# Token mix in three-pass fp32: the half tile of tokens is multiplied with all 128 rows, with zeros in two copies of its weights

## The chip, the cores and the metric

The kernel runs on one core of a Trainium2 chip (all four batches on that core). The metric is the device time of one launch in microseconds. A run with the profiler on gives the times of single instructions; from it come the span (first to last instruction) and the profiled execution's own time.

## The reference, cut to what matters

Three layers stand behind each other: a windowed attention (4 batches, 8 heads, 576 tokens), a channel mix of 512 channels, and a mixer block. The change is in the first half of the mixer block, the token mix:

```python
# x: (4 batches, 576 tokens, 512 channels)
xt = x.transpose(0, 2, 1)
h = np.maximum(xt @ w_tok1, 0.0) @ w_tok2      # w_tok1: 576 x 256, w_tok2: 256 x 576
u = x + h.transpose(0, 2, 1)
h2 = np.maximum(u @ w_ch1, 0.0) @ w_ch2        # 512 x 1536 and 1536 x 512
return u + h2
```

The first product sums over the 576 tokens of a batch. With tokens on the 128 partitions that is four and a half tiles.

## The kernel before, in words

**Arithmetic.** Every large product is made of three matmuls (`mm3`): each operand is split into a high part, rounded to the matmul's input type, and a low part, the rest (`split`: a copy, which the planner gives to ScalarE or VectorE, and a subtraction on VectorE). High times high, high times low and low times high are added up in one PSUM bank.

**Tokens and tiles.** The result of the channel mix lies in 18 tiles `x2[0..17]` of 128 tokens by 512 channels, the batches behind each other. Two batches are nine tiles: four for the even one, four for the odd one, and the ninth, whose rows 0 to 63 are the even batch's last 64 tokens and whose rows 64 to 127 the odd one's. `tiles_of(b)` lists the five tiles of a batch with the rows that count and the number of the weight block.

**Token mix.** `tokens_in(b)` splits each of the five tiles into a pair from the rings `x2h_r`, `x2l_r` (three pairs of 512 columns in z) and multiplies it with w_tok1: 2 halves of the hidden units by 3 matmuls of 512 columns, so 30 matmuls in two banks. For the fifth tile they have 64 rows of the contraction; there are 24 such over the four batches. The weights of the fifth tile lie in `t1[4]`, the tail of w_tok1 twice, once in rows 0 to 63 and once in rows 64 to 127. Then a ReLU gives `hid`. `turn(t)` transposes a tile into `wv` (TensorE, a bank, copies), and `tokens_out(b)` multiplies `hid` with w_tok2 (`t2`, slot at0): 8 groups of 6 matmuls of 288 columns, by turns in banks 6 and 7, each added into `wv` by VectorE. Behind that come the products with w_ch1 (`c1`) and w_ch2 (`c2`).

**Weights.** The weights come as 64-bit words. `weight` loads a block into a raw slot, makes fp32 of it by one ScalarE and three VectorE operations in a temporary slot, and splits it into its high and low place. For w_tok1, w_tok2 and the first four blocks of w_ch1 the raw slots are xt4 and xt5 by turns (`raw_b`), the temporary ones xt6 and xt7 (`tmp_b`). So there are two chains of blocks, the even one over xt4 and xt6, the odd one over xt5 and xt7. The later blocks of w_ch1 and w_ch2 go over wr0 to wr2 and z5 (`raw_c`, `tmp_c`), and wr3, xt4 to xt7 are taken afterwards by the split of u (`uhl_r`).

**What sets the order.** All operations go to a planner (class `Plan`), which records them (so all of them have one line in the profile, L392) and lists them per engine: each gets a due time, worked back from TensorE's own order with a table of costs, and of those that are ready the one with the earliest due time is taken. Two operations that share cells of a slot keep their order. So a change of places or sizes moves instructions on every engine.

The code that sets the places of the token mix:

```python
t1 = [pair(p, (HID,)) for p in cut("at", (1, 2), 512) + [("at", 0, 4 * S), ("at", 0, 4 * S + 512)]]
raw_b, tmp_b = ring(cut("xt", (4, 5), 512)), ring(cut("xt", (6, 7), 512))
x2h_r, x2l_r = ring(z512[9::2]), ring(z512[10::2])
```

Here z512 is z0 to z4 cut into 15 places of 512 columns; z512[8] is the last third of z2, and before the change the token mix doesn't use it.

Of the kernel before, what the change touches and what calls it, by code (L numbers as in the profile page):

```python
# [10 lines left out]
F32R = mybir.dt.float32r  # L11
# [7 lines left out]
B, H, S, D = 4, 8, 576, 64  # L19
C = H * D  # L20
NT = B * S
FF, HID, FF2 = 1024, 256, 1536
# [383 lines left out]
def tile_model(nc, banks, units, cst, mu, w_k, w_v, w_r, w_t1, w_t2, w_c1, w_c2, outT):  # L406
    memory = {k: [Slot(f"{k}{i}", n) for i, n in enumerate(v)] for k, v in SLOTS.items()}

    def f(view):
        return view.bitcast(F32)  # L410

    def at(place, shape, dtype=F32):
        name, number, offset = place
        return memory[name][number].view(offset, shape, dtype)
# [6 lines left out]
    def cut(name, numbers, size, count=None):  # L421

        out = []
        for n in numbers:
            out += [(name, n, size * i) for i in range(SLOTS[name][n] // size)]
        return out[:count]

    def ring(*places):
        return Ring(at, sum((p if isinstance(p, list) else [p] for p in places), []))

    def psum(*numbers):
        return Ring(bank, numbers)

    def mm3(out, lh, ll, rh, rl, first, last):

        nc.tensor.matmul(out=out, lhsT=lh, rhs=rh, start=first, stop=False)
        nc.tensor.matmul(out=out, lhsT=lh, rhs=rl, start=False, stop=False)
        nc.tensor.matmul(out=out, lhsT=ll, rhs=rh, start=False, stop=last)

    def copy(out, in_):  # L440
        nc.either(
            ("scalar", "activation", dict(out=out, in_=in_, func=AF.Copy)),
            ("vector", "tensor_copy", dict(out=out, in_=in_)),
        )

    def combine(out, in0, in1, op):
        nc.vector.tensor_tensor(out=out, in0=in0, in1=in1, op=op)

    def split(raw, hi, lo):
        copy(hi, raw)  # L450
        combine(lo, raw, f(hi), ALU.subtract)

    def rows(n):
        return slice(128 * n, 128 * n + 128)
# [6 lines left out]
    def pair(place, shape):  # L461

        name, number, offset = place
        n = int(np.prod(shape))
        return at(place, shape, F32R), at((name, number, offset + n), shape, F32R)
# [3 lines left out]
    wr = [pair(("wr", k, 0), (C,)) for k in range(4)]  # L469
# [3 lines left out]
    def words(w):  # L473
        return w.bitcast(U32)
# [2 lines left out]

        return words(w).rearrange("(k p) c -> p k c", p=128)[:, :, 2 * n * m:2 * n * m + 2 * n]

    def weight(srcs, hi, lo, raw_ring, tmp_ring):  # L480

        shape = tuple(hi.shape[1:])
        n = int(np.prod(shape))  # L490
        flat = raw_ring.tile(2 * n, dtype=U32)
        for part, src in srcs:
            dst = flat[part]
            if len(src.shape) == 3:
                dst = dst.split(src.shape[1], src.shape[2])
            nc.sync.dma_start(out=dst, in_=src)
            if raw_ring is raw_a:
                nc.early[len(nc.ops) - 1] = 6
        raw = flat.split(n, 2)
        low, h = raw[:, :, 0], raw[:, :, 1]  # L500
        t = tmp_ring.tile(n)
        b, half = t.bitcast(U32), t.bitcast(U16)
        v = nc.vector
        nc.scalar.activation(out=t, in_=f(h), func=AF.Copy, scale=2.0 ** -112)
        v.tensor_scalar(out=h, in0=b, scalar1=3, scalar2=None, op0=ALU.logical_shift_left)
        v.scalar_tensor_tensor(
            out=b, in0=b, scalar=0x80000000, in1=h, op0=ALU.bitwise_and, op1=ALU.bitwise_or
        )
        v.scalar_tensor_tensor(
            out=half, in0=low, scalar=2.0 ** -29, in1=half, op0=ALU.mult, op1=ALU.add  # L510
        )
        if len(shape) == 2:
            t = t.split(*shape)
        split(t, hi, lo)
# [4 lines left out]
    def weight_k(m):  # L519

        weight([(everything, col_block(w_k, m, 256))], *wk2[m], raw_a, tmp_a)

    def weight_r(kt):
        weight([(everything, words(w_r)[rows(kt), :])], *wr[kt], raw_a, tmp_a)

    def weight_v(m):

        two = words(w_v)[256 * m:256 * m + 256, :].rearrange("(k p) c -> p k c", p=128)
        weight([(everything, two)], *wv2[m], raw_a, tmp_a)
# [88 lines left out]
    z512 = cut("z", range(5), 512)  # L618
# [4 lines left out]
    x2 = [at(place, (C,)) for place in x2_at]  # L623
# [63 lines left out]
    def mix(c, m, j):  # L687
# [16 lines left out]
        out=om_sb, in0=mu_sb, scalar1=-1.0, scalar2=1.0, op0=ALU.mult, op1=ALU.add  # L704
    )
    diag = []
    for which in range(2):
        diag.append([])
        for kt in range(4):
            diag[which].append([])  # L710
            for k, factor in enumerate((om_sb, mu_sb)):
# [3 lines left out]
                        out=d, in0=ident, scalar1=factor[:, col], scalar2=None, op0=ALU.mult)),  # L715
# [19 lines left out]
    for g in range(8 * nchunk + 2):  # L735
        c, m = divmod(g, 8)
# [29 lines left out]
            attend(h, s_ring, t_ring, x_ring)  # L766


    t1 = [pair(p, (HID,)) for p in cut("at", (1, 2), 512) + [("at", 0, 4 * S), ("at", 0, 4 * S + 512)]]
    t2 = [pair(p, (S,)) for p in cut("at", (0,), 2 * S, 2)]  # L770
    raw_b, tmp_b = ring(cut("xt", (4, 5), 512)), ring(cut("xt", (6, 7), 512))
    for k in range(4):
        weight([(everything, words(w_t1)[rows(k), :])], *t1[k], raw_b, tmp_b)
    tail = words(w_t1)[512:576, :]
    weight([(slice(0, 64), tail), (slice(64, 128), tail)], *t1[4], raw_b, tmp_b)
    for k in range(2):
        for n in range(3):
            cs = slice(192 * n, 192 * n + 192)
# [12 lines left out]
    x2h_r, x2l_r = ring(z512[9::2]), ring(z512[10::2])  # L791
# [4 lines left out]
    def weight_1(m):  # L796
        if m < 4:
            for n in range(2):
                q = slice(2 * n, 2 * n + 2)
                weight([(everything, col_block(w_c1, m)[:, q, :])], c1[m][0][:, q, :], c1[m][1][:, q, :], raw_b, tmp_b)  # L800
        else:
            weight([(everything, col_block(w_c1, m))], *c1[m], raw_c, tmp_c)
# [3 lines left out]

    def tiles_of(b):
        base, odd = 9 * (b // 2), b % 2
        out = [(base + 4 * odd + i, slice(0, 128), i) for i in range(4)]
        return out + [(base + 8, slice(64 * odd, 64 * odd + 64), 4)]  # L810

    for m in range(4):
        weight_1(m)
    hid = {}
    hp_r, x2p_r, up_r = psum(0, 1, 2, 3), psum(4, 5), psum(6, 7)

    def tokens_in(b):
        hp = [hp_r.tile(C) for _ in range(2)]
        for n, (t, r, kt) in enumerate(tiles_of(b)):
            h, l = x2h_r.tile(C, dtype=F32R), x2l_r.tile(C, dtype=F32R)  # L820
            split(x2[t][r], h[r], l[r])
            for m in range(2):
                mm3(hp[m], t1[kt][0][r, rows(m)], t1[kt][1][r, rows(m)], h[r], l[r], n == 0, n == 4)
        hid[b] = []
        for m in range(2):
            h, l = (hid_r.tile(C, dtype=F32R) for _ in range(2))
            nc.scalar.activation(out=h, in_=hp[m], func=AF.Relu)
            nc.vector.scalar_tensor_tensor(
                out=l, in0=hp[m], scalar=0.0, in1=f(h), op0=ALU.max, op1=ALU.subtract
            )  # L830
            hid[b].append((h, l))
# [25 lines left out]
    for t in range(4):  # L857
        turn(t)
    tokens_in(0)
    turn(8)  # L860
    for t in range(4, 8):
        turn(t)
    tokens_in(1)
    tokens_out(0)
    for t in range(9, 13):
        turn(t)
    tokens_in(2)
    turn(17)
    tokens_out(1)
# [59 lines left out]
    for g in range(12 * nchunk + 2):  # L929
        c, m = divmod(g, 12)  # L930
# [90 lines left out]
```

## Time and profile before

| | us |
|---|---|
| median of 3 runs | 734.55 |
| lowest, highest | 733.45, 735.19 |
| profiled execution, its own time | 732.79 |
| span of the profiled execution | 731.0 |
| TensorE busy in the span | 715.6 (98%) |
| VectorE busy | 404.7 (55%) |
| ScalarE busy | 287.1 (39%) |

The granted clock of TensorE, as a mean over the span, is 0.989 of full. The token mix lies between 362 and 430 us of the span. In TensorE's timeline a row gives its start and length; rows of like neighbours are joined. The length of a row runs past the start of the next one, since matmuls overlap, so an instruction's price is read from start to start.

### The profile page before, as it was taken

The numbers are of one execution on the slowest core, as the hardware profiler recorded it, in microseconds if no ns is written. First come the engines' busy times: TensorE is split into PE (matmuls) and PEld (weight loads), VectorE is DVE, ScalarE is ACT, GpSimd is POOL, SyncE is SP. The second block draws the span as 40 slices with busy tenths as digits, with TensorE's granted clock in tenths as the row PEclk, the third lists the DMA queues.
The fourth block names the chain that finished last, engine by engine and source line by source line (L and its number), as shares of the span: only waits on it lengthen the run. The fifth ranks groups of instructions, "written<-read, shape, count | busy, mean of one in ns | idle before, by whom it ended". The sixth has DMA issues, their size and how long they took to land.

```text
span 731.0 us, 10615 instructions
## 1 busy us (share of the span) xinstructions
PE 715.6 (98%) x4124; PEld 604.6 (83%) x4124; DVE 404.7 (55%) x917; ACT 287.1 (39%) x803; POOL 1.2 (0%) x20
## 2 busy tenths in 40 slices
PE   7699999999999999999999999999999999999998
PEld 6578888888888888988878888888888888888897
DVE  6898898387477388786788898132114112211121
ACT  5776775356244354464466543120112011011110
POOL 0000000000000000000000000000000000000000
PEclk9799999999999999999999999999999999999999
DMA  8946632214122100203321342001000000100010
GB/s 293 323 156 225 196 132 81 67 52 144 47 68 70 46 16 22 73 30 105 98 81 54 96 127 76 1 0 58 1 0 23 35 1 1 57 1 0 1 59 30
DMA packets 26082, 53.84 MB, mean 74 GB/s; under 512 B 2480, under 2 KB 10032, under 8 KB 26032
## 3 DMA queue, kind: packets, MB, share of 16 engines
q1 hardware_dynamic: 26032, 53.17, 22.9%
q8 instruction: 32, 0.52, 0.3%
q14 instruction: 18, 0.15, 0.1%
HBM read 48.44 MB, written 4.72 MB: 73 GB/s over the span
## 4 chain that ended last, share of the span: by engine, by line
PE 95%; DMA 4%; SPq 0%; issue 0%; DVE 0%
PE bank L392 95%; DMA at<-units 2%; DMA wr<-units 1%; DMA wv<-units 1%; SPq L392 0%; DVE z L392 0%
## 5 line engine op out<-in xcount | busy, mean ns | idle before, releaser
L392 PE MATMUL bank<-z,wk 128*128 128x384 f32 (+2 forms) x816 | 196.4, 358 | 0.0
L392 DVE SCALAR_TENSOR_TENSOR z<-bank,z 128x512 fp32r<-128x512 f32 (+2 forms) x116 | 70.4, 607 | 222.3 <-ACT z L392 221.5
L392 ACT ACTIVATE z<-bank 128x512 fp32r<-128x512 f32 (+3 forms) x123 | 65.0, 529 | 285.3 <-PE bank L392 284.3
L392 PEld LDWEIGHTS bank<-z,wk 128*128 128x128 f32 x816 | 146.9, 188 | 15.1 <-ACT x L392 0.3
L392 PE MATMUL bank<-wv,z 128*128 128x512 f32 x432 | 128.9, 405 | 0.0
L392 PE MATMUL bank<-z,x 128*128 128x512 f32 (+1 forms) x540 | 120.2, 371 | 0.0
L392 PEld LDWEIGHTS bank<-z,x 128*128 128x128 f32 x540 | 94.9, 188 | 18.7
L392 PEld LDWEIGHTS bank<-wv,z 128*128 128x128 f32 x432 | 78.3, 189 | 13.8
L392 PE MATMUL bank<-z,at 128*128 128x512 f32 (+2 forms) x300 | 76.9, 388 | 0.0
L392 PE MATMUL bank<-wr,z 128*128 128x512 f32 x216 | 62.8, 406 | 0.0
L392 PEld LDWEIGHTS bank<-z,at 128*128 128x128 f32 (+1 forms) x300 | 52.6, 188 | 11.3 <-issue 1.3
L392 PE MATMUL bank<-at 128*128 128x96 f32 (+1 forms) x252 | 46.3, 284 | 11.0 <-DMA at<-cst 4.9
L392 ACT ACTIVATE at<-bank,at 128x96 f32<-128x96 f32 x128 | 42.4, 340 | 23.7 <-PE bank L392 11.6
L392 DVE TENSOR_TENSOR z<-z,z 128x384 fp32r<-128x384 f32 x88 | 48.1, 554 | 5.8 <-ACT z L392 2.6
L392 PE MATMUL bank<-xt,wk 128*128 128x512 f32 (+2 forms) x176 | 45.2, 387 | 0.0
L392 PEld LDWEIGHTS bank<-wr,z 128*128 128x128 f32 x216 | 39.2, 189 | 6.6
L392 PEld LDWEIGHTS bank<-at 128*128 128x128 f32 x216 | 35.3, 195 | 8.0 <-DMA at<-units 4.1
L392 PE MATMUL bank<-at,z 128*128 128x288 f32 x192 | 35.9, 306 | 0.0
L392 PEld LDWEIGHTS bank<-xt,wk 128*128 128x128 f32 x176 | 30.5, 192 | 6.1
L392 ACT ACTIVATE z<-z 128x384 fp32r<-128x384 f32 x57 | 29.5, 522 | 14.3 <-DVE z L392 8.3
L392 ACT ACTIVATE x<-bank 96x512 f32<-96x512 f32 (+1 forms) x41 | 24.2, 594 | 27.1 <-PE bank L392 26.9
L392 PEld LDWEIGHTS bank<-at,z 128*128 128x128 f32 x192 | 29.7, 188 | 4.0 <-issue 1.8
(106 smaller groups left out, 787.2 us busy)
## 6 DMA issues: line engine op xcount, KB each, us to landing
at<-units SPq DMA_DIRECT2D x27, 416.0 KB, 3.7
wr<-w_c SPq DMA_DIRECT2D x20, 512.0 KB, 3.6
at<-units SPq DMA_DIRECT2D x27, 192.0 KB, 2.6
x<-w_k SPq DMA_DIRECT2D x4, 1024.0 KB, 6.9
x<-w_v SPq DMA_DIRECT2D x4, 1024.0 KB, 7.0
wv<-units SPq DMA_DIRECT2D x8, 416.0 KB, 6.6
outT<-z SPq DMA_DIRECT2D x9, 256.0 KB, 2.0
x<-w_r SPq DMA_DIRECT2D x4, 512.0 KB, 3.6
```

The lines of the kernel that those rows point to most:

```text
L392: call(kw["out"], kw["constant"]) if method == "memset" else call(**kw)
```

## The change

`weight` gets a parameter `zero`: the rows it names are set to zero in the raw slot, by a memset on GpSimd. The tail of w_tok1 becomes two blocks in place of one: `t1[4]` with the tail in rows 0 to 63 and zeros below, `t1[5]` with zeros in rows 0 to 63 and the tail below. The sixth pair lies in z512[8]. The fifth tile of a batch is multiplied with all 128 rows, by `t1[4]` for an even batch and `t1[5]` for an odd one. Its split is made for all 128 rows, once for two batches, at a place in wr3 (`ends`), no longer in the rings.

```diff
+        if zero is not None:
+            nc.gpsimd.memset(out=f(flat[zero]), constant=0.0)
...
-    t1 = [pair(p, (HID,)) for p in cut("at", (1, 2), 512) + [("at", 0, 4 * S), ("at", 0, 4 * S + 512)]]
+    t1 = [pair(p, (HID,)) for p in cut("at", (1, 2), 512) + [("at", 0, 4 * S), ("at", 0, 4 * S + 512), z512[8]]]
...
-    weight([(slice(0, 64), tail), (slice(64, 128), tail)], *t1[4], raw_b, tmp_b)
+    halves = [slice(0, 64), slice(64, 128)]
+    for odd in range(2):
+        weight([(halves[odd], tail)], *t1[4 + odd], raw_b, tmp_b, zero=halves[1 - odd])
...
-        out = [(base + 4 * odd + i, slice(0, 128), i) for i in range(4)]
-        return out + [(base + 8, slice(64 * odd, 64 * odd + 64), 4)]
+        return [(base + 4 * odd + i, i) for i in range(4)] + [(base + 8, 4 + odd)]
...
-        for n, (t, r, kt) in enumerate(tiles_of(b)):
-            h, l = x2h_r.tile(C, dtype=F32R), x2l_r.tile(C, dtype=F32R)
-            split(x2[t][r], h[r], l[r])
+        for n, (t, kt) in enumerate(tiles_of(b)):
+            if n < 4:
+                h, l = x2h_r.tile(C, dtype=F32R), x2l_r.tile(C, dtype=F32R)
+            elif b % 2 == 0:
+                h, l = ends[b // 2] = at(("wr", 3, 0), (C,), F32R), at(("wr", 3, 512), (C,), F32R)
+            else:
+                h, l = ends[b // 2]
+            if n < 4 or b % 2 == 0:
+                split(x2[t], h, l)
             for m in range(2):
-                mm3(hp[m], t1[kt][0][r, rows(m)], t1[kt][1][r, rows(m)], h[r], l[r], n == 0, n == 4)
+                mm3(hp[m], t1[kt][0][:, rows(m)], t1[kt][1][:, rows(m)], h, l, n == 0, n == 4)
```

The order of the instructions moves with it. TensorE, half tile of batch 3 (z3, z4, wr3: halves of the tile, the moving operand; at0, z2: weights of the tail; the rows on bank6 and bank7 are tokens_out of batch 2), before:

```order
L392 MATMUL bank7_68<-at0_1_2633,z0_0_526 128x288 x2
L392 MATMUL bank2_63<-z3_0_474,at0_1_2633 128x512
L392 MATMUL bank7_68<-at0_1_2633,z0_0_526 128x288
L392 MATMUL bank2_63<-z4_1_532,at0_1_2633 128x512
L392 MATMUL bank7_68<-at0_1_2633,z0_0_526 128x288 x2
L392 MATMUL bank2_63<-z3_0_474,at0_1_2633 128x512
L392 MATMUL bank7_68<-at0_1_2633,z1_0_580 128x288
L392 MATMUL bank3_64<-z3_0_474,at0_1_2633 128x512
L392 MATMUL bank3_64<-z4_1_532,at0_1_2633 128x512
L392 MATMUL bank3_64<-z3_0_474,at0_1_2633 128x512
L392 MATMUL bank6_67<-at0_1_2633,z0_0_526 128x288 x5
```

The same place after:

```order
L392 MATMUL bank7_68<-at0_1_2628,z0_0_526 128x288 x2
L392 MATMUL bank2_63<-wr3_1_585,z2_0_434 128x512
L392 MATMUL bank7_68<-at0_1_2628,z0_0_526 128x288
L392 MATMUL bank2_63<-wr3_1_585,z2_0_434 128x512
L392 MATMUL bank7_68<-at0_1_2628,z0_0_526 128x288 x2
L392 MATMUL bank2_63<-wr3_1_585,z2_0_434 128x512
L392 MATMUL bank7_68<-at0_1_2628,z1_0_580 128x288
L392 MATMUL bank3_64<-wr3_1_585,z2_0_434 128x512 x3
L392 MATMUL bank6_67<-at0_1_2628,z0_0_526 128x288 x5
```

The sequence is the same, matmul for matmul; the half tile's operands come from wr3 and z2, with all rows.

SyncE's queue, loads of the token mix's weights (xt4, xt5: raw slots; w_t1, w_t2, w_c1, w_c2: w_tok1, w_tok2, w_ch1, w_ch2), before:

```order
L392 DMA xt4_0_83<-w_t1 64x512 x2
L392 DMA xt5_0_85<-w_t2 128x384
L392 DMA xt4_0_83<-w_t2 128x384
L392 DMA xt5_0_85<-w_t2 128x384
L392 DMA xt4_0_83<-w_t2 128x384
L392 DMA xt5_0_85<-w_t2 128x384
L392 DMA xt4_0_83<-w_t2 128x384
L392 DMA xt5_0_85<-w_c1 128x2x256
L392 DMA xt4_0_83<-w_c1 128x2x256
L392 DMA xt5_0_85<-w_c1 128x2x256
```

The same place after:

```order
L392 DMA xt4_0_83<-w_t1 64x512
L392 DMA xt5_0_85<-w_t1 64x512
L392 DMA xt4_0_83<-w_t2 128x384
L392 DMA xt5_0_85<-w_t2 128x384
L392 DMA xt4_0_83<-w_t2 128x384 x2
L392 DMA xt4_0_83<-w_c1 128x2x256 x4
L392 DMA wr2_2_3096<-w_c1 128x4x256
L392 DMA wr0_2_3112<-w_c2 128x1024
L392 DMA wr1_2_3128<-w_c2 128x1024
L392 DMA xt5_0_85<-w_t2 128x384 x2
L392 DMA wr0_2_3112<-w_c2 128x1024
L392 DMA xt5_0_85<-w_c1 128x2x256
```

The loads of xt5 move behind those of xt4 and behind three of wr.

ScalarE, at the last chunk of the channel mix (x24, x25: tiles of its result; z5 to z4: the mix of the last chunk; xt6, xt7: temporary slots of the two chains), before:

```order
L392 ACTIVATE x24_0_188<-bank0_61 128x512
L392 ACTIVATE xt6_0_79<-xt4_0_83 128x256
L392 ACTIVATE z5_0_513<-bank1_62 128x384
L392 ACTIVATE xt7_0_81<-xt5_0_85 128x256
L392 ACTIVATE xt2_1_3122<-xt6_0_79 128x256
L392 ACTIVATE z4_1_532<-z5_0_513 128x384
L392 ACTIVATE z3_0_474<-x25_0_685 128x512 x2
L392 ACTIVATE x24_0_188<-bank2_63 128x512
```

The same place after:

```order
L392 ACTIVATE x24_0_188<-bank0_61 128x512
L392 ACTIVATE xt6_0_79<-xt4_0_83 128x256
L392 ACTIVATE z5_0_513<-bank1_62 128x384
L392 ACTIVATE z2_0_434<-xt7_0_81 128x256
L392 ACTIVATE z4_1_532<-z5_0_513 128x384
L392 ACTIVATE z3_0_474<-x25_0_685 128x512
L392 ACTIVATE xt7_0_81<-xt5_0_85 128x192
L392 ACTIVATE z3_0_474<-x25_0_685 128x512
L392 ACTIVATE x24_0_188<-bank2_63 128x512
```

The odd chain is at its second tail block (the write into z2) and its first piece of w_tok2 where it was at the last pieces of w_ch1.

## Rows read from the trace of the kernel before

**Rows 1.** The page: busy time of each engine, chain that ended last.

```profile
PE 715.6 (98%) x4124; PEld 604.6 (83%) x4124; DVE 404.7 (55%) x917; ACT 287.1 (39%) x803; POOL 1.2 (0%) x20
PE 95%; DMA 4%; SPq 0%; issue 0%; DVE 0%
```

**Rows 2.** TensorE's timeline, half tile of batch 3 (start us, us, engine, operands).

```profile
415.27 0.42 PE L392 MATMUL bank<-at,z 128*128 128x288 f32 x2
415.62 0.50 PE L392 MATMUL bank<-z,at 64*128 64x512 f32 x1
...
416.38 0.49 PE L392 MATMUL bank<-z,at 64*128 64x512 f32 x1
...
418.01 0.97 PE L392 MATMUL bank<-z,at 64*128 64x512 f32 x3
418.91 1.86 PE L392 MATMUL bank<-at,z 128*128 128x288 f32 x12
420.61 0.86 PE L392 MATMUL bank<-xt,xt 128*128 128x512 f32 x3
```

**Rows 3.** TensorE's timeline, two stretches of like matmuls.

```profile
426.44 1.75 PE L392 MATMUL bank<-at,z 128*128 128x288 f32 x12
428.04 0.39 PE L392 MATMUL bank<-wr,xt 128*128 128x512 f32 x1
...
485.31 2.92 PE L392 MATMUL bank<-z,at 128*128 128x512 f32 x12
488.07 2.94 PE L392 MATMUL bank<-z,xt 128*128 128x512 f32 x12
```

**Rows 4.** Its ends of the stretches of batches 0, 1, 2; the form's group.

```profile
369.11 1.59 PE L392 MATMUL bank<-z,at 128*128 128x512 f32 x5
...
372.12 0.76 PE L392 MATMUL bank<-cst,x 128*128 128x128 f32 x5
372.64 1.18 PE L392 MATMUL bank<-z,at 128*128 128x512 f32 x4
...
379.85 1.76 PE L392 MATMUL bank<-z,at 128*128 128x512 f32 x6
...
384.49 0.38 PE L392 MATMUL bank<-cst,x 128*128 128x128 f32 x2
...
396.34 1.75 PE L392 MATMUL bank<-z,at 128*128 128x512 f32 x6
...
399.28 0.27 PE L392 MATMUL bank<-cst,x 128*128 128x128 f32 x1
...
L392 PE MATMUL bank<-z,at 64*128 64x512 f32 x24 | 8.8, 444 | 0.0
```

**Rows 5.** Windows: us, busy PE, PEld, DVE, ACT, POOL, PEclk, DMA share, GB/s.

```profile
343.00:362.00 19.00, 19.00 (x97) 16.64 (x96) 13.07 (x28) 7.72 (x16) 0.00 (x0) 1.00 0.35 112
362.00:430.00 68.00, 68.00 (x392) 57.00 (x391) 58.82 (x111) 42.13 (x95) 0.00 (x0) 1.00 0.28 86
430.00:470.00 40.00, 40.00 (x174) 32.50 (x173) 25.74 (x48) 12.90 (x22) 0.00 (x0) 1.00 0.23 67
```

**Rows 6.** TensorE's timeline: last receptance matmul; first tokens_out matmuls.

```profile
344.71 0.40 PE L392 MATMUL bank<-wr,z 128*128 128x512 f32 x1
...
376.88 0.42 PE L392 MATMUL bank<-at,z 128*128 128x288 f32 x2
```

**Rows 7.** Groups by form, whole span (busy, mean ns; idle before, releaser).

```profile
L392 DVE TENSOR_TENSOR z<-x,z 64x512 fp32r<-64x512 f32 x4 | 2.7, 685 | 0.4 <-ACT z L392 0.4
L392 DVE SCALAR_TENSOR_TENSOR xt<-xt,xt 128x256 uint16<-128x256 uint32 x13 | 5.6, 450 | 0.2
L392 POOL MEMSET xt<- 128x1 f32 x16 | 1.1, 111 | 57.1 <-PE bank L392 56.8 <-POOLq L1005 0.3
```

**Rows 8.** The page: DMA issues (count, KB each, median us to landing).

```profile
wr<-w_c SPq DMA_DIRECT2D x20, 512.0 KB, 3.6
xt<-w_t SPq DMA_DIRECT2D x6, 192.0 KB, 2.4
```

More of the change, by code (lines that the diff above doesn't have):

```diff
@@ L478, in col_block, with weight @@
         return words(w).rearrange("(k p) c -> p k c", p=128)[:, :, 2 * n * m:2 * n * m + 2 * n]
-    def weight(srcs, hi, lo, raw_ring, tmp_ring):
+    def weight(srcs, hi, lo, raw_ring, tmp_ring, zero=None):
         shape = tuple(hi.shape[1:])
@@ L808, in tiles_of @@
         base, odd = 9 * (b // 2), b % 2
-        out = [(base + 4 * odd + i, slice(0, 128), i) for i in range(4)]
-        return out + [(base + 8, slice(64 * odd, 64 * odd + 64), 4)]
+        return [(base + 4 * odd + i, i) for i in range(4)] + [(base + 8, 4 + odd)]
     for m in range(4):
         weight_1(m)
-    hid = {}
+    hid, ends = {}, {}
     hp_r, x2p_r, up_r = psum(0, 1, 2, 3), psum(4, 5), psum(6, 7)
```

## The prediction

> **What bounds the kernel now.** I read the page first, for the engine that sets the end. TensorE is busy for 98% of the span and the chain that ended last is 95% TensorE [rows 1]. Then I read the windows over the stretch that the change touches, 343 to 430 us: TensorE is busy 19.00 of 19 us and 68.00 of 68, at a granted clock of 1.00 [rows 5]. It never waits there, so only what makes its own instructions take less time, or what makes it wait for the first time, can move the end. Busy time alone does not say what an instruction costs, since the records of neighbours overlap. So I read TensorE's timeline from start to start.
>
> In a stretch of like instructions the price is steady. Twelve 512-column matmuls take 485.31 to 488.07, which is 0.230 us each; twelve of 288 columns take 426.44 to 428.04, 0.133 each [rows 3]. Now the half tile of batch 3 [rows 2]. A 64-row matmul starts at 415.62, and after one 288-column matmul of 128 rows the next 64-row one starts at 416.38. That pair takes 0.76 us where 0.230 + 0.133 = 0.363 would do: 0.40 us too much. The extra time is not in the 64-row matmul as such: three of them in a row take 418.01 to 418.91, 0.90 us for 0.69, so 0.21 too much on three; the rest of the 0.4 falls on the neighbours of 128 rows. It hangs on the passage from 128 rows to 64 and back. The reader is to see a fixed price for each run of 64-row matmuls, however long the run.
>
> **The change, part by part.**
>
> *The half tiles get all 128 rows.* The 24 matmuls stay 24, of 512 columns each [rows 4]; there is none less. But no run of 64 rows is left, so all passages go. The sum, stretch by stretch, is start to start less what the same instructions cost in the uniform stretches. (A row of the timeline joins neighbours and carries the form of the first; the order of the program gives the counts within.)
> - Batch 3, 415.27 to 420.61: 5.34 us. In it 18 matmuls of 288 columns and 6 of 512: 18 × 0.133 + 6 × 0.230 = 3.77. Excess 1.57, in 4 runs [rows 2].
> - Batch 1, 379.85 to 384.49: 4.64 us, with 8 of 512 and 12 of 288, 3.44. Excess 1.20, in 3 runs [rows 4].
> - Batch 2, 396.34 to 399.28: 2.94 us, with 7 of 512 and 4 of 288, 2.14. Excess 0.80, in 2 runs [rows 4].
> - Batch 0, 369.11 to 372.64: 3.53 us, with 7 of 512 (1.61) and 8 transposes. Five transposes at the end take 372.12 to 372.64, 0.104 each, so 0.83. Excess 1.09, in 3 runs [rows 4].
>
> Together 4.66 us for 12 runs, 0.39 a run; I take 4.65. It lies wholly on the path, since TensorE does nothing else in that time. What could make it smaller is that 128 rows cost more than 64 in themselves. Within the run of three the price is that of a full matmul plus one passage, so I take none. The bounds are all of the excess, and half of it, if only one side of each passage vanished.
>
> The Trainium skill, "TensorEngine Tiling (Array Packing)", section "Theoretical Speedup", says that a contraction of 64 rows or fewer can run up to twice as fast when the array is split into tiles. By that rule a 64-row matmul would be worth 0.115 us less than a full one, and the 24 would lose 2.8 us of the gain by being widened. The row of three at 418.01 shows no such halving [rows 2]. So the sum goes by the row; the rule stands among the rivals.
>
> *One split per pair of batches.* Four half-tile splits become two. Each removed one saves 0.685 us of VectorE [rows 7] and a copy on ScalarE or VectorE. TensorE waits for none of them, so it is worth nothing by itself; it is relief for VectorE of 1.37 us.
>
> *A second copy of the tail weights.* The tail is loaded as two single pieces in place of two parts of one slot, so no byte is added; there is one more conversion (one ScalarE operation, three on VectorE, a copy and a subtraction). Each is at most 0.45 us by the dearest of its kind [rows 7], except that the subtraction of 256 columns lies below the 0.685 of 512. It comes on ScalarE and VectorE while TensorE is busy throughout [rows 5]. Cost 0 with that cover; without it, some 2.25 us once.
>
> *Two memsets of 64x512 on GpSimd.* No such memset is in the trace. From below: 0.11 us for 128x1 [rows 7]; from above: 0.685 us, what VectorE takes for a subtraction of 64x512 [rows 7], doubled for a slower engine, 1.4. I take 1.0, near the upper end, since the form is that of the upper row. GpSimd has nothing else here, and the load of the other half of the same slot, of 128 KB, lasts some 2.4 us by the row of 192 KB [rows 8], so the cost is 0 at either end.
>
> *A wait that is new.* The second copy lies in a part of z2 that holds an operand of the last receptance. Its last matmul starts at 344.71 and takes 0.40 [rows 6], so the copy can be written from about 345.1. Behind it hangs one of the two chains of raw and temporary buffers: three of the six pieces of w_tok2, then four halves of the first w_ch1 blocks. On ScalarE the conversion of the mix and two tile copies for batch 0 stand behind the waiting copy; in SyncE's queue two of the three pieces now stand behind three 512 KB loads of wr.
> When are they ready? The copy and subtraction end by 346.4 (2 × 0.685 at most). Three wr loads add 3.6 us [rows 8]. A step of the chain is a load of 2.4 [rows 8] and five operations of at most 0.45 [rows 7], 2.25: some 4.7 us. So 346.4 + 3.6 + 3 × 4.7 = 364.1. The first tokens_out matmul, which reads w_tok2, starts at 376.88 [rows 6], and at 375.8 when batch 0 has lost its 1.09. There are 11.7 us to spare; cost 0, and if the cover were gone, whatever the steps exceed.
>
> *VectorE in 362 to 430.* It is busy 58.82 of 68.00 us [rows 5]. The four halves of w_ch1 that come later bring at most 4 × 4 × 0.45 = 7.2 us, the removed splits take away 1.37: 64.65. The stretch shrinks to 68.00 − 4.65 = 63.35. So it would be 1.3 us over full. Much of that work, though, converts blocks of w_ch1 and w_ch2 that are used later, and in 430 to 470 VectorE is busy only 25.74 of 40 [rows 5]. I take it to slip there, cost 0. This is the weakest step: an addition of tokens_out that stands behind two conversions in the queue would hold a PSUM bank, and TensorE with it.
>
> **The sum.** The profiled execution took 732.79 us (span 731.0) and lies 1.76 below the median of 734.55. Less 4.65 it would be 728.1 (span 726.35). The median becomes 734.55 − 4.65 = 729.9; from the lowest and highest run, 728.8 and 730.5.
>
> **The rivals.**
> 1. VectorE gives part of it back. For it: 64.65 us of work in 63.35. Against it: less than that is urgent. It gives back 1.3 us at least; if the queue also stands still for a twentieth of a stretch of some 35 us around tokens_out, 3. Time 731.2 to 732.9.
> 2. Only one side of each passage vanishes, or the wider matmul costs something. For it: no row shows a 128-row half tile. Against it: the uniform rows. Half of 4.65 stays: 732.2.
> 3. A 64-row matmul is in truth cheaper, by half, and its price is hidden behind the passages. The change then gains 4.65 − 24 × 0.115 = 1.9: 732.7. Against it: the row of three. This is what the rule of the Trainium skill above would do.
> 4. Slower. The second copy's wait starves tokens_out. The chain must be later than 375.8: from 346.4 + 3.6 that is a step of over 8.6 us; the whole gain is lost over 10.2. At 11 us a step TensorE waits 383 − 375.8 = 7.2, and the time is 734.55 + 2.55 = 737.1. For it: three more transfers ahead in the queue, and VectorE nearly full. Against it: a step by rows is 4.7.
> 5. More gain than summed: the first matmuls of other stretches also change neighbours, or the relief of ScalarE counts. 728.5.
> That the change does nothing on TensorE is excluded by the order: none of its rows there is a 64-row one.
>
> **How the numbers follow.** Chances: forecast 0.69, rival 1 0.19, rival 2 0.04, rival 3 0.02, rival 4 0.04, rival 5 0.02. The forecast with the spread of the runs covers 728.8 to 730.5; I let the range begin at 728.6 and reach to 732.5, which takes in most of rivals 1 and 2 and leaves about 0.15 outside. Within 0.2% (1.5 us) is about what a measurement of this kernel can tell from no change; 733.1 is that bound. Faster is nearly all of the forecast and of rivals 1, 2, 3 and 5: 0.90. Same is a rival 1 that gives back over 3 us, or rival 4 near its turning point: 0.06. Slower 0.04.
>
> **What would show it.** In the changed profile TensorE's timeline should show 0.230 and 0.133 us start to start through tokens_in of all four batches, and no row with 64 rows. The four stretches should take 3.77, 3.44, 2.14 and 2.44 us. TensorE should be busy throughout 343 to 425. Wrong would be: idle time on TensorE ahead of the first tokens_out matmuls, released by VectorE on at0 (rival 4) or on a bank that a VectorE addition frees (rival 1); or half-tile matmuls more than 0.235 us apart in a stretch of their like (rivals 2, 3).

## The result, and the profile after

The changed kernel took 728.32 us (median of 4 runs, 727.19 to 728.68) against 734.87 for the kernel before in the same comparison: ratio 0.9911, 95% interval 0.9893 to 0.9929. That is 6.5 us less where 4.65 were forecast, and 0.3 us below the range. In two later comparisons with more runs the ratio was 0.9925 (0.990 to 0.995) and 0.9937 (0.9917 to 0.9956); the forecast 4.65 us is 0.9937. How much of the first difference lay in the runs of before is told apart below.

The page of the profile after: span, busy time of each engine, chain that ended last. They answer to [rows 1].

```profile
span 725.4 us, 10621 instructions
PE 709.9 (98%) x4124; PEld 604.4 (83%) x4124; DVE 405.3 (56%) x922; ACT 285.3 (39%) x800; POOL 2.3 (0%) x22
PE 94%; DMA 3%; DVE 1%; ACT 0%; SPq 0%; issue 0%
```

TensorE has the same 4124 matmuls and 5.7 us less busy time. Its timeline through the half tile of batch 3 in the changed kernel (start us, us, operands), which answers to [rows 2]:

```profile
411.25 0.43 PE L392 MATMUL bank<-at,z 128*128 128x288 f32 x2
411.52 0.39 PE L392 MATMUL bank<-wr,z 128*128 128x512 f32 x1
411.75 0.29 PE L392 MATMUL bank<-at,z 128*128 128x288 f32 x1
411.88 0.39 PE L392 MATMUL bank<-wr,z 128*128 128x512 f32 x1
...
412.74 0.86 PE L392 MATMUL bank<-wr,z 128*128 128x512 f32 x3
413.43 1.75 PE L392 MATMUL bank<-at,z 128*128 128x288 f32 x12
415.02 0.63 PE L392 MATMUL bank<-xt,xt 128*128 128x512 f32 x2
```

From 411.52 to 411.88 a 512-column and a 288-column matmul take 0.36 us, where the pair with 64 rows took 0.76. The whole stretch, 411.25 to 415.02, takes 3.77 us, to the hundredth what the sum had for it; before it took 5.34.

Windows of the changed kernel (us, busy PE, PEld, DVE, ACT, POOL, granted clock, DMA share, GB/s), which answer to [rows 5]:

```profile
343.00:362.00 19.00, 19.00 (x99) 16.66 (x98) 14.79 (x35) 9.02 (x22) 0.00 (x0) 1.00 0.47 145
362.00:425.40 63.40, 63.40 (x389) 57.11 (x388) 58.14 (x118) 41.57 (x96) 0.00 (x0) 1.00 0.29 88
```

TensorE still does not wait. VectorE is busy for 58.14 of 63.40 us: fuller than before (58.82 of 68.00), but not full.

To tell the token mix from everything else I take two fixed points of TensorE's timeline: the last matmul of the receptance, ahead of the token mix, and a run of twelve matmuls (the first on at0 as a weight of w_ch2) behind it. In the profile before they stand at 344.71 [rows 6] and 485.31 [rows 3], 140.60 us apart. After:

```profile
343.73 0.40 PE L392 MATMUL bank<-wr,z 128*128 128x512 f32 x1
...
479.70 2.92 PE L392 MATMUL bank<-z,at 128*128 128x512 f32 x12
```

They are 135.97 us apart, 4.63 less. The remaining 0.98 of the 5.6 us between the two profiles lies ahead of the first point. Matched instruction by instruction, the two timelines part by it within the first 100 us, where both programs have the same instructions in the same order on every engine, and by no more from there to the first point.

| stretch of the half tile | before, us | summed for after | measured after |
|---|---|---|---|
| batch 0 | 3.53 | 2.44 | 2.50 (368.15 to 370.65) |
| batch 1 | 4.64 | 3.44 | 3.47 (377.83 to 381.30) |
| batch 2 | 2.94 | 2.14 | 2.13 (393.15 to 395.28) |
| batch 3 | 5.34 | 3.77 | 3.77 (411.25 to 415.02) |

### The profile page after: what moved, and what is told of

It is laid out like the page before. It is cut to its first block, busy times and chain, and to the rows that moved or that the text cites. A ratio compares the mean times of both kernels' runs of the same rounds, so it can differ in the third digit from the quotient of the medians.

```text
span 725.4 us, 10621 instructions
## 1 busy us (share of the span) xinstructions
PE 709.9 (98%) x4124; PEld 604.4 (83%) x4124; DVE 405.3 (56%) x922; ACT 285.3 (39%) x800; POOL 2.3 (0%) x22
## 4 chain that ended last, share of the span: by engine, by line
PE 94%; DMA 3%; DVE 1%; ACT 0%; SPq 0%; issue 0%
PE bank L392 94%; DMA x<-w_v 1%; DMA wr<-units 1%; DMA wv<-units 1%; DVE x L392 1%; SPq L392 0%; DVE at L392 0%; ACT x L392 0%; ACT wk L392 0%; DVE z L392 0%; ACT at L392 0%
## 5 line engine op out<-in xcount | busy, mean ns | idle before, releaser
L392 PE MATMUL bank<-z,at 128*128 128x512 f32 (+1 forms) x276 | 68.9, 383 | 0.0
L392 PE MATMUL bank<-wr,z 128*128 128x512 f32 x228 | 66.6, 406 | 0.0
L392 PEld LDWEIGHTS bank<-z,at 128*128 128x128 f32 x276 | 48.4, 188 | 8.6
L392 PEld LDWEIGHTS bank<-wr,z 128*128 128x128 f32 x228 | 41.4, 189 | 7.0
```

Source lines behind the costliest of these rows:

```text
L392: call(kw["out"], kw["constant"]) if method == "memset" else call(**kw)
```

## The experiments

Theory A: a passage between matmuls of 64 and of 128 rows has a fixed price, some 0.39 us for a run of 64-row matmuls, and that is the whole gain. Rivals: the single split or the moved chains bring a part; the 64-row matmul itself is dear; or the change also shortens the start.

The distance between the two fixed points, from one profile of each kernel, carries most of the verdicts:

| kernel | first point | second | distance | against before |
|---|---|---|---|---|
| before, first profile | 344.71 | 485.31 | 140.60 | |
| before, second profile | 346.81 | 488.95 | 142.14 | +1.54 |
| before, third profile | 344.87 | 485.44 | 140.57 | -0.03 |
| changed, first profile | 343.73 | 479.70 | 135.97 | -4.63 |
| changed, second profile | 343.68 | 479.89 | 136.21 | -4.39 |
| changed, third profile | 343.34 | 479.30 | 135.96 | -4.64 |
| changed, 64 rows again | 346.68 | 487.23 | 140.55 | -0.05 |
| before, full rows alone | 346.18 | 482.17 | 135.99 | -4.61 |
| before, runs of six | 347.06 | 484.54 | 137.48 | -3.12 |
| before, all tiles 64 rows | 344.98 | 513.55 | 168.57 | +27.97 |
| the same in 8 runs | 345.12 | 483.87 | 138.75 | -1.85 |
| paired halves | 347.17 | 482.24 | 135.07 | -5.53 |
| paired halves, early | 344.33 | 478.38 | 134.05 | -6.55 |

### 1. Both kernels once more

No edit.

> The kernel before once more, unchanged, for the spread of the first 100 us, where both kernels run the same instructions and the profile after is nevertheless 0.97 us ahead. Theory A, chance of the start: this profile too is shifted against the first one of before by some tenths of a us up to 1 us within the first 100 us and by nothing after that; ratio 1.000. Theory B, the start belongs to the program: the shift in the first 100 us is under 0.1 us and the ratio is 1.000.

> The changed kernel once more, unchanged. Theory A, only the passages count and the rest of the measured 6.5 us was the start: in more rounds the ratio comes down towards 0.9937 (4.65 us less), and this profile is 4.64 us shorter than before between 362 and 435 us, with another shift in the first 100 us. Theory B, the change also makes the start shorter: the ratio stays at 0.991 (6.5 us less) and the first 100 us are again about 1 us shorter.

Measured: the kernel before 733.25 us (12 runs) against 733.98 (29 runs) for itself, ratio 0.9995 (0.9974 to 1.0016); the changed one 728.49 (6 runs), ratio 0.9925 (0.990 to 0.995). The first point, ahead of the token mix, stood at 344.71 in the first profile of before and at 346.81 in the second: the same program starts 2.1 us later or earlier. That is theory A of the start, though beyond the 1 us it allowed. The ratio of the changed kernel lies between its two theories, and its start was again 1 us ahead, as theory B wanted; number 7 comes back to it.

The second profile of before had something else, which neither theory foresaw. Two fixed points are 142.14 us apart, 1.54 too many. Windows behind the half tile of batch 3 in it:

```profile
400.00:420.00 20.00, 20.00 (x121) 17.21 (x120) 16.67 (x33) 12.61 (x30) 0.00 (x0) 1.00 0.32 95
420.00:422.00 2.00, 2.00 (x8) 1.47 (x8) 1.65 (x3) 1.61 (x4) 0.00 (x0) 0.75 0.34 114
422.00:424.00 2.00, 2.00 (x10) 2.00 (x9) 1.05 (x2) 0.10 (x1) 0.00 (x0) 0.50 0.00 0
```

and the timeline rows in it, TensorE, with the last 64-row run and what follows:

```profile
420.11 0.97 PE L392 MATMUL bank<-z,at 64*128 64x512 f32 x3
421.02 3.25 PE L392 MATMUL bank<-at,z 128*128 128x288 f32 x12
424.06 1.04 PE L392 MATMUL bank<-xt,xt 128*128 128x512 f32 x3
```

The twelve 288-column matmuls take 3.04 us from start to start where they took 1.70 in the first profile [rows 2]. The granted clock stood at 0.50, the lower of its two levels (1.2 GHz in place of 2.4). It came down after four runs of 64-row matmuls in 5 us, and TensorE never waited.

### 2. The changed kernel with 64 rows again

```diff
-                mm3(hp[m], t1[kt][0][:, rows(m)], t1[kt][1][:, rows(m)], h, l, n == 0, n == 4)
+                r = slice(0, 128) if n < 4 else halves[b % 2]
+                mm3(hp[m], t1[kt][0][r, rows(m)], t1[kt][1][r, rows(m)], h[r], l[r], n == 0, n == 4)
```

> The changed kernel with its two copies, its single split and its order of loads, but the half tile multiplied with 64 rows again. Theory A, the passages between 64 and 128 rows are the gain: 12 runs of 64-row matmuls are back, so 4.65 us come back, 362 to 435 us as long as before, ratio about 1.000. Rival, the single split and the moved chains bring a part of the gain: ratio 0.994 to 0.997, and the stretch stays 2 to 4 us shorter than before.

Measured: 733.76 us (12 runs), ratio 1.000 (0.9979 to 1.0021); the distance is 140.55, as before. The single split, the second copy and the moved chains are all in this kernel, and none of the gain is. TensorE at batch 3 of it:

```profile
417.58 0.50 PE L392 MATMUL bank<-wr,z 64*128 64x512 f32 x1
418.01 0.40 PE L392 MATMUL bank<-at,z 128*128 128x288 f32 x1
418.34 0.49 PE L392 MATMUL bank<-wr,z 64*128 64x512 f32 x1
```

The pair takes 0.76 us again, now with the operands in wr3 and z2: the price belongs to the rows, not to the place.

### 3. The kernel before with full rows alone

```diff
-        return out + [(base + 8, slice(64 * odd, 64 * odd + 64), 4)]
+        return out + [(base + 8, slice(0, 128), 4)]
```

> The kernel before with its order and its one copy of the tail weights, but each half tile split and multiplied with all 128 rows, so that both batches' last tokens go into the sum of either: the separation of the two batches is left out. Theory A, the passages alone: 4.65 us less between 362 and 435 us as in the changed kernel, ratio 0.9937. Rival, the second copy and the moved chains bring part of it: less than 4 us.

Measured: 729.40 us (4 runs), ratio 0.9937 (0.9918 to 0.9956), distance 135.99. With 2 it closes the question from both sides: rows alone give 4.61 us, and all the rest of the change moves the distance by no more than 0.05 us.

### 4. Runs of six

```diff
+            start = len(nc.ops)
             for m in range(2):
                 mm3(hp[m], t1[kt][0][r, rows(m)], t1[kt][1][r, rows(m)], h[r], l[r], n == 0, n == 4)
+            if n == 4:
+                nc.burst(start)
```

> The kernel before with the six 64-row matmuls of a batch kept together, so 4 runs of six in place of 12 runs; nothing else is changed. Theory A, a fixed price of 0.39 us a run: 8 x 0.39 = 3.1 us less, ratio 0.9957. Rival, each 64-row matmul costs 0.19 us more than one of 128 rows: no gain, ratio 1.000.

Measured: 730.41 us (12 runs), ratio 0.9952 (0.9937 to 0.9967), distance 137.48: 3.12 less, against 8 x 0.39 = 3.1 expected. TensorE at the half tile of batch 0 in it:

```profile
371.32 0.49 PE L392 MATMUL bank<-cst,x 128*128 128x128 f32 x3
371.74 1.66 PE L392 MATMUL bank<-z,at 64*128 64x512 f32 x6
373.33 0.77 PE L392 MATMUL bank<-cst,x 128*128 128x128 f32 x5
```

Six 64-row matmuls from 371.74 to 373.33 take 1.59 us for 6 x 0.230 = 1.38: 0.21 too much for six, as for three and for one. The price hangs on the run, not on the matmul; the rival of a dear 64-row matmul falls.

### 5. All tiles by 64 rows: does the clock come down?

```diff
-        out = [(base + 4 * odd + i, slice(0, 128), i) for i in range(4)]
+        out = [(base + 4 * odd + i, slice(64 * odd, 64 * odd + 64), i) for i in range(4)]
```

> The kernel before with all five tiles of each batch multiplied by 64 rows only (rows 0 to 63 for an even batch, 64 to 127 for an odd one), so half of the tokens are left out of the first product; the number and order of the matmuls stay. Theory A, 0.39 us a run: 47 runs in place of 12, 35 x 0.39 = 13.7 us more, ratio 1.019, with the granted clock at 1.00 from 362 to 430. Theory C, 64-row matmuls also bring the granted clock down, as it stood at 0.50 behind batch 3 in the second profile of before: the clock lies at 0.50 in one or more stretches between 362 and 430 us, and the kernel is slower by 16 us or more, ratio 1.022 or above.

Measured: 765.46 us (4 runs, 761.01 to 775.00, with mean granted clocks from 0.969 down to 0.951), ratio 1.0436 (1.0391 to 1.048). The profiled run is the shortest, with 28 us more between the fixed points where 35 runs more would cost 13.7. Windows of it:

```profile
362.00:380.00 18.00, 18.00 (x78) 11.48 (x78) 13.37 (x24) 12.34 (x30) 0.00 (x0) 1.00 0.19 59
380.00:400.00 20.00, 20.00 (x78) 14.14 (x77) 11.09 (x22) 8.91 (x18) 0.00 (x0) 0.74 0.08 26
400.00:420.00 20.00, 20.00 (x71) 14.08 (x71) 10.49 (x20) 8.05 (x17) 0.00 (x0) 0.74 0.26 79
420.00:450.00 30.00, 30.00 (x116) 20.53 (x115) 17.20 (x32) 11.00 (x24) 0.00 (x0) 0.77 0.23 71
450.00:480.00 30.00, 30.00 (x150) 25.41 (x149) 27.61 (x55) 13.30 (x23) 0.00 (x0) 1.00 0.35 106
```

The clock lay at its full level up to 380, had a mean of 0.74 to 0.77 for 70 us, and was full again behind the token mix. In these 70 us (380 to 450) the lost clock alone is 20 x 0.26 + 20 x 0.26 + 30 x 0.23 = 17.3 us, where 28.0 - 13.7 = 14.3 are to be explained. The sum does not close to better than 3 us, but by either count the clock accounts for half of the 28 us or more.

### 6. The same matmuls in 8 runs: rows or passages?

```diff
+        for part in (range(3), range(3, 5)):
...
+            start = len(nc.ops)
+            for n, (r, kt, h, l) in pairs.items():
+                for m in range(2):
+                    mm3(hp[m], t1[kt][0][r, rows(m)], t1[kt][1][r, rows(m)], h[r], l[r], n == 0, n == 4)
+            nc.burst(start)
```

> The kernel with all five tiles on 64 rows (half the tokens left out, as there), but the 30 matmuls of a batch kept in one run of 18 and one of 12, so 8 runs in place of 47. If the granted clock falls because of the 64 rows, it lies at 0.50 in some stretch between 362 and 430 us here too, and the kernel is 5 us or more slower than before. If it falls because of the passages, which stop the tensor engine for 0.2 us each, it stays at 1.00 and the kernel is 4 x 0.39 = 1.6 us faster than before.

Measured: 731.35 us (8 runs), ratio 0.997 (0.9954 to 0.9987), distance 138.75: 1.85 less than before, where four runs fewer would give 1.6. TensorE's timeline, then the windows of it:

```profile
362.59 4.39 PE L392 MATMUL bank<-z,at 64*128 64x512 f32 x18
366.90 1.09 PE L392 MATMUL bank<-cst,x 128*128 128x128 f32 x8
367.93 4.42 PE L392 MATMUL bank<-z,at 64*128 64x512 f32 x18
```

```profile
362.00:380.00 18.00, 18.00 (x87) 13.48 (x86) 17.31 (x30) 14.17 (x32) 0.00 (x0) 1.00 0.28 81
380.00:400.00 20.00, 20.00 (x130) 17.75 (x129) 18.54 (x36) 14.51 (x35) 0.00 (x0) 1.00 0.21 66
400.00:420.00 20.00, 20.00 (x124) 17.52 (x123) 18.41 (x36) 13.24 (x29) 0.00 (x0) 1.00 0.43 131
```

Eighteen 64-row matmuls in a row cost 0.239 each (4.31 / 18, their passage included), and the clock stayed full, with as many 64-row matmuls as in 5; its mean over the span lay between 0.988 and 0.991 in all eight runs. So 64 rows as such do not bring the clock down here; 64 rows together with many passages do.

### 7. The changed kernel and the kernel before, a third time

> The changed kernel a third time, for the first 100 us. Chance: its profile is shifted against the first one of before by 0 to +2.5 us in the first 100 us. The program: it is ahead by about 1 us again.

> The kernel before once more, for the first 100 us and for the clock behind the half tile of batch 3. Chance of the start: shifted by 0 to +2.5 us against the first profile in the first 100 us. The clock: a stretch at 0.50 behind 415 us, costing some 1.5 us, is there in one profile of two by what was seen.

Measured: the changed kernel 728.80 us (6 runs) against 733.20 (11 runs), ratio 0.9937 (0.9917 to 0.9956), 4.4 us less. Its profile was ahead at the first point by 1.37 us. The kernel before took 734.09 (10 runs), ratio 1.0008 (0.9993 to 1.0022), and its third profile lies within 0.2 us of the first at both points. So the first point lay between 343.3 and 343.7 in three profiles of the changed kernel, and between 344.7 and 347.2 in the others but one (the last row of the table, 344.33). The granted clock tells them apart. Every profile has a stretch at the lower level in its start. Windows of the first profile of before, then of the changed kernel:

```profile
38.00:40.00 2.00, 2.00 (x6) 0.95 (x4) 1.98 (x2) 1.73 (x4) 0.00 (x0) 0.56 0.49 141
38.00:40.00 2.00, 1.66 (x31) 0.97 (x31) 1.98 (x3) 2.00 (x6) 0.00 (x0) 1.00 0.65 227
```

From 38 to 40 us the clock is at 1.00 in all three profiles of the changed kernel and at 0.56, 0.50 and 0.71 in the three of before. It is at 0.50 there in experiment 2 too, which has all of the changed kernel's instructions up to the token mix in the same order, and its first point stood at 346.68. So the same instructions can also start late. And the profiled run of the changed kernel was the shortest in each comparison (727.19 of 727.19 to 728.68; 727.39 of 727.39 to 730.28; 726.80 of 726.80 to 731.09), with a mean clock of 0.992 or 0.993, which only one of its 13 other runs had. Its three profiles show its better starts; nothing shows that the program as such starts sooner.

The clock's stretch at 0.50 behind 415 us, which was given one chance in two, is not in the third profile of before.

### 8. Two halves side by side

```diff
+        start = len(nc.ops)
+        for m in range(2):
+            for w, x in ((0, h), (0, l), (1, h)):
+                for odd in range(2):
+                    r = slice(64 * odd, 64 * odd + 64)
+                    nc.tensor.matmul(
+                        out=sums[b - 1 + odd][m], lhsT=t1[4][w][r, rows(m)], rhs=x[r], start=False, stop=w == 1
+                    )
+        nc.burst(start)
```

(The odd batch's `tokens_in` calls this behind its four tiles, with one split of the ninth tile and the one copy of weights of the kernel before; the hidden units of both batches follow.)

> The kernel before with the half tiles of two batches multiplied in one run of twelve: 64-row matmuls of the even batch (rows 0 to 63) and of the odd one (rows 64 to 127) by turns, into different banks. There are 2 runs in place of 12. Theory A with two 64-row matmuls one behind the other: 10 x 0.39 = 3.9 us less than before, ratio 0.9947, 0.8 us behind the changed kernel. Rival, the rule that two matmuls of 64 rows run side by side: a run of twelve takes 1.4 us in place of 2.76, so 2.8 us less again, 6.7 us less than before, ratio 0.9909, 2 us ahead of the changed kernel. Against both: the hidden units of the even batch come later, and tensor idle time before tokens_out takes some back.

Measured: 729.46 us (6 runs), ratio 0.9937 (0.9919 to 0.9955); distance 135.07, 5.53 less than before and 0.9 less than the changed kernel. By run time it is no faster than the changed kernel in the same comparison (728.80 us, the same ratio). The matmuls did run side by side (shown below on the next kernel), but TensorE waited behind them. TensorE, the first tokens_out of the kernel, with the idle time ahead and its releaser in brackets:

```profile
380.70 0.54 PE L392 MATMUL bank<-at,z 128*128 128x288 f32 x2 [0.20 <-ACT z L392]
381.63 0.80 PE L392 MATMUL bank<-at,z 128*128 128x288 f32 x4 [0.39 <-DVE z L392]
```

The idle time is 0.59 us together; no idle time in TensorE's timeline answers to the second figure of the next expectation, 0.68.

The next version moves the pairs behind the odd batch's first tile and tells the planner's table of costs that the second of a pair is free:

```diff
+            if b % 2 and n == 0:
+                halves(tiles_of(b)[4][0], b - 1)
+                hidden(b - 1)
...
+                nc.ops[-1]["tensor"] = (*nc.ops[-1]["tensor"][:2], 0.003)
```

> As the paired halves, but the run of twelve stands behind the odd batch's first tile in place of its last one, and the list of costs by which the order is made counts the second of each pair as free, so that other matmuls stand between the even batch's sums and the tokens_out that waits for them. Theory: the waits of 0.59 and 0.68 us on the hidden units, seen behind the first run of twelve, are gone; 2 runs in place of 12 and 12 pairs in place of 24: 3.9 + 2.8 = 6.7 us less than before between 362 and 435 us, ratio 0.9909, ahead of the changed kernel by 2 us. Rival: the waits come back at another place, 5.5 us as for the paired halves.

Measured: 726.59 us (6 runs, 725.37 to 727.89), ratio 0.990 (0.9882 to 0.9919); distance 134.05, 6.55 less than before and 1.92 less than the changed kernel. It has the lowest time of all, but it was not timed beside the changed kernel, and the intervals of the two ratios overlap (0.9917 to 0.9956 there); the 1.92 us rests on one profile of each. TensorE at its first run of twelve:

```profile
370.89 0.27 PE L392 MATMUL bank<-cst,x 128*128 128x128 f32 x1
371.09 1.65 PE L392 MATMUL bank<-z,at 64*128 64x512 f32 x12
372.68 0.98 PE L392 MATMUL bank<-cst,x 128*128 128x128 f32 x7
```

Twelve 64-row matmuls of 512 columns take 1.59 us, as six of them took in experiment 4. Two matmuls with different row halves share the time of one. TensorE is busy for all of the 68 us from 362 to 430: the waits are gone.

## Why the prediction was right and where it was wrong

**The passages: right, to 0.02 us.** The sum had 4.65 us for 12 runs; the profiles show 4.63 and 4.64 (and once 4.39, where 0.25 us went around 357 us, ahead of the token mix). Full rows alone give 4.61, 64 rows put back give 0.05, four runs in place of twelve give 3.12. The step from rows of a trace to a price per run held, and so did the reading that the price is on the neighbours and does not grow with the run (one, three, six, eighteen matmuls).

**The single split and the tail's second conversion: right, nothing.** TensorE does not wait in 343 to 425 us.

**The memsets: mis-sized, without effect.** I took 1.0 us between 0.11 and 1.4; the profile after shows 0.519 each (groups by form):

```profile
L392 POOL MEMSET xt<- 64x512 f32 x2 | 1.0, 519 | 226.4 <-DVE xt L392 226.4
```

**The wait of the second copy: right in the result, wrong in its steps.** The last of three late pieces of w_tok2 was to be ready by 364.1 at the latest. VectorE's timeline shows the subtraction that ends the second copy, and the three that end the pieces:

```profile
342.76 0.42 DVE L392 TENSOR_TENSOR z<-xt,z 128x256 fp32r<-128x256 f32 x1
...
346.06 0.36 DVE L392 TENSOR_TENSOR at<-xt,at 128x192 fp32r<-128x192 f32 x1
...
352.89 0.35 DVE L392 TENSOR_TENSOR at<-xt,at 128x192 fp32r<-128x192 f32 x1
...
358.54 0.35 DVE L392 TENSOR_TENSOR at<-xt,at 128x192 fp32r<-128x192 f32 x1
```

The last ends at 358.89; the first tokens_out matmul starts at 374.87. Rival 4 (slower) was 16 us away. But the sum had 4.7 us for a step, with five operations where the kernel's words name six (one on ScalarE, three on VectorE, a copy and a subtraction), and 3.6, the time of one load, for three. The two steps that had a load in them took 6.8 and 5.7 us. The sum held because the second copy ended at 343.18 in place of 346.4 and the first piece, whose load was in already, followed within 3.2 us.

**VectorE: right in the result.** I counted up to 64.65 us of work in 63.35 and took the excess to slip behind 430. In the window there are 58.14 us, and from 425.4 to 465.4 VectorE is busy for 29.03 us, where the 40 us behind 430 had 25.74 [rows 5]: the work did slip. Nothing was given back (rival 1).

**The rival by the rule of tiling: right and wrong.** By the rule, a contraction of 64 rows can run up to twice as fast; I set it aside because three such matmuls in a row took 0.90 us. All three used the same row half. With row halves by turns, twelve take 1.59 us: the rule holds, but here only for neighbours with different halves, which the half tiles of the kernel before never had. So the change as such loses nothing by widening, and the kernel with the shortest token mix doesn't widen. The Trainium skill, "TensorEngine Tiling (Array Packing)", section "Key Properties", says both: different tiles can run in parallel, and changing the mode drains the engine. The traces agree as far as they go, with 1.59 us for twelve and 0.39 us for each run: they show what a passage costs, not what the engine does in it.

**What failed: the base of the sum and the range.** The step is "The median becomes 734.55 − 4.65 = 729.9; from the lowest and highest run, 728.8 and 730.5". The saving was right, the base was not. Three runs had to stand for a kernel whose time varies by several us. The profiled execution, 732.79 us, already lay 0.66 below the lowest of the three; less 4.65 it gives 728.1, and the range, from 728.6, left that out. Over all comparisons the kernel before was timed 85 more times: median 733.76, from 731.7 up. Less 4.65, that is 729.1; the changed kernel's 16 runs have a median of 728.52, so the measured difference is 5.24 us. The rest, 0.6 us, goes with the clock. Of the 85 runs 23 had a mean granted clock of 0.988 or less, with a median of 735.05; the other 62 have 733.06. Of the changed kernel's 16 runs two were such, and the other 14 have 728.44. Like with like: 733.06 - 728.44 = 4.62 us. That it comes so near to 4.65 is partly luck, since the cut was chosen after the runs were seen: from 0.989 to 0.991 the two medians differ by 4.8 us (733.43 and 728.62), from 0.992 up by 4.9 (732.22 and 727.29).

So the passages cost the kernel before 0.39 us each time, in every run. A second cost is seen, but not how often it comes: a fall of the clock. One profile of three shows it, right behind the half tile of batch 3, for a loss of 1.54 us; experiment 5 has more passages and several such stretches, and 6 has fewer and none. Kernels with 12 scattered runs (before and experiment 2) had 25 of 97 runs at a mean clock of 0.988 or less, those with none to eight (the changed one, and experiments 3, 4, 6 and 8) had 4 of 52. Whether this fall is what sets those runs apart is not shown. The comparisons ran on several chips, on which the share of such runs differed; on one of them it was 1 of 11 against 2 of 16. Of these 29 runs only one was profiled (0.986), and it had a late start as well: the clock was still at 0.50 from 40 to 42 us, where the first and third profile of before were at 1.00. The prediction had "more gain than summed" at 0.02, for other reasons; this mechanism is in no part of it, and that its 728.5 lies near the measured time is luck.

Rival 2 (half of the price stays) fell with the table of stretches: no more than 0.06 us is left in any.

## What to carry to other kernels

When TensorE is back to back, read its timeline from start to start and compare unlike neighbours with uniform stretches: a fixed loss at each change of the contraction's row count shows there, and not as idle time. Then either pad to 128 rows, or keep the 64-row matmuls together, or let two row halves with different banks take turns, which had the shortest token mix here, since two cost one; and put other matmuls between their sums and who reads them. A saving is best forecast as a difference between like runs: three runs are too few for a base when the start of the program varies by 2 us.

## What the runs showed of the hardware

- A run of 64-row matmuls between 128-row ones cost 0.39 us on the mean of twelve runs of one to five, wherever the operands lay (at0 and z, or wr3 and z2), and 0.37 on the mean of four runs of six (137.48 less 135.99, by 4).
- Two neighbouring matmuls of 64 rows with different row halves and different banks ran side by side: twelve of 512 columns in 1.59 us. With the same half they took 0.23 to 0.24 each.
- TensorE's granted clock fell to 0.50 in the middle of a program, in a stretch in which TensorE never waited, behind scattered runs of 64-row matmuls: once in three profiles of the kernel before with its 12 runs, for a loss of 1.54 us, and to a mean of 0.74 to 0.77 over 70 us with 47 runs. With as many 64-row matmuls in 8 runs it stayed at 1.00.
- The same program reached the last matmul of its receptance between 344.7 and 346.8 us in three profiles of before; the difference arose in the first 100 us, and the latest had the clock at 0.50 longest in its start (still from 40 to 42 us).
